# Storing the rows of three late attention steps from other buffers, on another DMA queue and at a later place

## The chip, the cores and the metric

The kernel runs on one core of one Trainium2 chip. A core has the engines TensorE (PE; its weight loads are listed as PEld), VectorE (DVE), ScalarE (ACT), GpSimd (POOL) and SyncE (SP). SP computes nothing here: it issues DMAs. ACT and POOL issue DMAs too; all of them are moved by the core's 16 DMA engines. The metric is the device time of one execution in microseconds (us), lower being better.

## The reference

Two blocks follow each other. The first is a linear attention with decay (4 batches, 8 heads, 768 positions, head size 64, blocks of 64), the second a mixture of experts that sends each of the 3072 tokens to one of 8 experts.

```python
for b in range(nb):                                   # attention
    intra = einsum('bhic,bhjc->bhij', qb, kb) * Dmask
    intra = einsum('bhij,bhjd->bhid', intra, vb)
    inter = einsum('bhid,bhde->bhie', qb * lam_pow, kv_state)
    out[:, :, sl] = intra + inter
    kv_state = lam_block * kv_state + einsum('bhsd,bhse->bhde', kb_dec, vb)
x = out.transpose(0, 2, 1, 3).reshape(B * S, H * D)   # 3072 x 512
logits = x @ w_gate
expert_idx = argmax(logits, axis=1)
for e in range(E):                                    # experts
    xe = x[expert_idx == e]
    h = maximum(xe @ w1[e], 0.0)                      # 512 x 1024
    out[expert_idx == e] = gate_w * (h @ w2[e])       # 1024 x 512
```

## The kernel before, in words

**Attention.** The loop over `steps` has 12 steps: step i handles block pair n = i // 2 (128 positions, of 6) of two batches. For each step q, k and v arrive by DMA from SP (512 KB each) in one of five buffers per name, the lists in `homes` (three of the pool `qkv`, two inside the rooms of the expert weights); step i uses buffer i % 5. PE turns q and k, forms scores and products, and keeps the running states. One step later `leave` turns the step's result into rows of x: `rows` writes them with ACT copies to `m.x`, one of the two slots of `x_room`, and `store_rows` stores these 512 KB to the DRAM tensor `xs` with one DMA from ACT's queue. The logits of the gate are formed beside this, `choose`, `ranks` and `put` give each token a place on its expert's list, and POOL writes the places into the DRAM tensor `slots` with small indirect DMAs ("puts", L467).

**Early start of the experts.** In step 8 `load_early` loads the first expert's w1 (`FIRST` is expert 5) in two DMAs of 1 MB from SP (L1121). `gather_early`, called in step 10, has POOL gather the first 256 rows of this expert's list from the rows that steps 0 to 7 stored (two indirect DMAs, L528, tile `list_0a`), held until the scores of step 11 are through. Behind them SP loads the expert's w2, 2 MB (L1140), with a dependency on both gathers:

```python
        behind = nc.sync.dma_start(out=w2t, in_=w2_r[FIRST])
        pin(behind)
        for other in begun:
            tc.add_manual_dep(behind.ins, other.ins.name, ...)
```

**Experts.** Pass "0a" (these 256 rows) starts while the last places are being given: `turn` (L593), `hidden` (L607, whose results ACT brings out at L560), then `outputs_early`. The product with w2 is done with seven block products instead of eight, from sums: `second_sums` has DVE form four sums of w2 (L684, tiles t_q, t_v, t_k, t_m), `left_of` four sums of the hidden rows (L753 to L756, tiles h_sd, h_qT, h_kT, h_kd), and `block` multiplies (L775): first two products with w2 itself, then t_k with h_kT, t_v with h_sd, and so on. Pass "0b" takes the rest of expert 5 (`list_0b`), and passes 1 to 7 take the other experts; the order of these is computed on the chip (`turns`), so SP reads `turns`, then each list (L497), then issues the loads of w1 (L202) and w2 (L204). The first other expert's rows are gathered by POOL (L528), cut into 16-bit planes by ACT (L576), turned by DMA transposes from SP (L578), joined by ACT (L586) and summed by DVE (L714); the gathers read all of `xs`, so they come after every store of rows.

**Order.** Each engine runs its instructions in order; `pin` keeps an instruction at its written place. All DMAs that SP issues stand in one queue, all that ACT issues in another, POOL's indirect ones in a third.

## Time and profile before

| | |
|---|---|
| median of 3 runs | 432.62 us (432.19 to 433.0) |
| profiled execution, its own time | 432.71 us |
| its span in the profile | 430.9 us |
| PE busy | 420.1 us (97% of the span) |
| PEld / DVE / ACT / POOL busy | 91% / 62% / 41% / 59% |
| granted TensorE clock, mean | 0.993 |
| DMA | 83.11 MB, 193 GB/s over the span |

The span is what the profiler sees from the first to the last instruction; 1.8 us of the execution's time lie around it. The profile names instructions by line, engine, output and input tile. "Idle before" an instruction is the time in which its engine did nothing just before it, put down to what ended last. A DMA's row on SPq or ACTq is its issue alone; the transfer itself shows in the waits for it and in the DMA share and GB/s of a stretch.

### The profile page before, as it was taken

To read this page: it belongs to the slowest core of one execution; us is meant where nothing else is said; L and a number is where in the kernel's file an instruction comes from. 1 tells how busy PE (TensorE), PEld (TensorE's weight loads), DVE (VectorE), ACT (ScalarE), POOL (GpSimd) and SP (SyncE) were. 2 spreads that over 40 slices of the span, in tenths; PEclk is the share of its full clock that TensorE was granted. 3 is DMA by queue.
4 is the path that set the end of the run, shared out by engine and by line. 5 is a ranking of instruction groups with operands and counts; after the bars stand their busy time and mean duration, and the time that the engine had idled before them with its cause. 6 is when DMAs were issued, how large, how long until landed. Compare 5 with 4: busy or idle time off the path is not lost.

```text
span 430.9 us, 9572 instructions
## 1 busy us (share of the span) xinstructions
PE 420.1 (97%) x3699; PEld 392.5 (91%) x3699; DVE 266.1 (62%) x585; ACT 176.7 (41%) x319; POOL 255.5 (59%) x204
## 2 busy tenths in 40 slices
PE   7999999999999999999999999999999999999993
PEld 5888998888888897999999999999999999999972
DVE  6656566676766547686557756665565564775463
ACT  3366546555542433450554155245424605422221
POOL 4242556472444367777948757693984887749032
PEclk8999999999999999999999999999999999999998
DMA  9999999999594759966378846956965894743121
GB/s 174 206 238 243 241 223 259 250 226 223 198 290 155 229 99 273 291 221 257 60 156 182 325 74 153 351 154 119 311 225 84 202 382 77 159 181 56 20 83 63
DMA packets 164551, 83.11 MB, mean 193 GB/s; under 512 B 145923, under 2 KB 145959, under 8 KB 164496
## 3 DMA queue, kind: packets, MB, share of 16 engines
q1 hardware_dynamic: 155024, 63.21, 61.0%
q0 software_dynamic: 5536, 12.88, 9.8%
q10 hardware_dynamic: 3936, 6.31, 4.2%
q8 instruction: 31, 0.51, 0.5%
q14 instruction: 24, 0.20, 0.2%
HBM read 58.96 MB, written 12.72 MB: 166 GB/s over the span
## 4 chain that ended last, share of the span: by engine, by line
PE 93%; ACT 1%; DVE 1%; DMA 1%; SPq 1%; issue 1%; POOL 0%; POOLq 0%
PE p L729 30%; PE p L915 26%; PE sp L279 6%; PE op L314 5%; PE ph L607 5%; PE p L775 4%; PE p L783 3%; PE tx L376 3%; PE cp L340 3%; PE op L305 2%; PE tk L241 2%; PE tq L241 2%; PE lgT L366 2%; DMA k_in<-in_k_dram 1%; ACT xT L332 1%; SPq L114 1%
## 5 line engine op out<-in xcount | busy, mean ns | idle before, releaser
L534 POOL DMA_INDIRECT out_dram<-o_room,list x24 | 25.2, 1048 | 52.2 <-DMA decay<-planes_q 28.3
L286 DVE TENSOR_TENSOR mt<-sp,decay 128x512 f32<-128x512 f32 x48 | 30.1, 684 | 22.4 <-PE sp L279 17.2
L740 ACT ACTIVATE hT<-hT 128x418 f32<-128x418 f32 (+6 forms) x56 | 28.3, 521 | 34.0 <-DVE hT L737 29.9
L729 PE MATMUL p<-xgT,w1t 128*128 128x209 f32 (+6 forms) x224 | 41.4, 327 | 0.0
L729 PEld LDWEIGHTS p<-xgT,w1t 128*128 128x128 f32 x224 | 37.1, 189 | 0.8 <-issue 0.8
L619 ACT COPY u_qT<-p 128x418 f32<-128x418 f32 (+6 forms) x14 | 6.7, 479 | 69.2 <-PE p L729 69.2
L915 PE MATMUL p<-hT,w2t 128*128 128x209 f32 (+5 forms) x192 | 33.6, 328 | 0.0
L915 PEld LDWEIGHTS p<-hT,w2t 128*128 128x128 f32 x192 | 32.0, 189 | 0.0
L528 POOL DMA_INDIRECT xg<-xs,list x25 | 26.3, 1053 | 9.0 <-issue 6.1
L467 POOL DMA_INDIRECT slots<-entry,slot_i x24 | 23.7, 990 | 11.8 <-PE tl L391 5.7
L737 DVE TENSOR_TENSOR hT<-p,u_kd 128x418 f32<-128x418 f32 (+6 forms) x28 | 15.7, 559 | 20.8 <-PE p L729 20.8
L279 PE MATMUL sp<-qT,kT 64*128 64x128 f32 x384 | 27.0, 289 | 0.1
L656 POOL TENSOR_TENSOR s_q<-w1t 128x1024 f32<-128x1024 f32 x7 | 16.5, 2363 | 16.8 <-DVE t_xT L714 14.8
L269 POOL TENSOR_TENSOR kd<-k_in,kdec 128x512 f32<-128x512 f32 x12 | 12.4, 1041 | 23.6 <-issue 10.7
L279 PEld LDWEIGHTS sp<-qT,kT 64*128 64x128 f32 x384 | 23.9, 196 | 2.6 <-issue 2.0
L607 PE MATMUL ph<-xgT,w1t 128*128 128x256 f32 (+1 forms) x128 | 21.6, 328 | 0.0
L326 ACT COPY xT<-op 128x512 f32<-128x512 f32 x12 | 7.0, 585 | 34.8 <-PE op L314 31.2
L586 ACT COPY xgT<-decay 128x1672 uint16<-128x1672 uint16 (+6 forms) x7 | 13.6, 1938 | 17.9 <-DMA decay<-planes_k 9.4
L607 PEld LDWEIGHTS ph<-xgT,w1t 128*128 128x128 f32 x128 | 19.2, 191 | 1.7
L729 PE MATMUL p<-t_sd,w1t 128*128 128x209 f32 (+6 forms) x112 | 20.7, 327 | 0.0
L729 PE MATMUL p<-st,s_q 128*128 128x209 f32 (+6 forms) x112 | 20.7, 327 | 0.0
L653 POOL TENSOR_TENSOR w1t<-w1t 128x1024 f32<-128x1024 f32 x7 | 20.3, 2901 | 0.6
(252 smaller groups left out, 1097.0 us busy)
## 6 DMA issues: line engine op xcount, KB each, us to landing
w2t<-in_moe_w_dram SPq DMA_DIRECT2D x8, 2048.0 KB
w1t<-in_moe_w_dram SPq DMA_DIRECT2D x7, 2048.0 KB
xs<-x_room ACTq DMA_DIRECT2D x12, 512.0 KB
v_in<-in_v_dram SPq DMA_DIRECT2D x8, 512.0 KB
o_room<-qs_room SPq DMA_DIRECT2D x76, 48.0 KB
q_in<-in_q_dram SPq DMA_DIRECT2D x7, 512.0 KB
k_in<-in_k_dram SPq DMA_DIRECT2D x7, 512.0 KB
room<-in_q_dram SPq DMA_DIRECT2D x4, 512.0 KB
```

The source lines that it names most:

```text
L241: pin(nc.tensor.transpose(t[:, i, b, :], src[:, b, h:h + 2, :], ident))
L279: m.scored = pin(nc.tensor.matmul(sp[u][:, i, b, :], lhsT=m.kT[s][halves[u], i, b, :], rhs=m.qT[s][halves[u], i, b, :], start=(i == 0 and ...
L286: nc.vector.tensor_mul(mt[:, u], sp[u], decay[:, u, s * HP // 2:(s + 1) * HP // 2].unsqueeze(2).to_broadcast(shp))
L314: pin(nc.tensor.matmul(out_at(m, b, u, hp), lhsT=m.v[:, b, 2 * hp + u, :], rhs=m.mt[hp // 2][:, u, hp % 2, b, :], start=(first and hp == 0 ...
L467: put = nc.gpsimd.indirect_dma_start(out=slots, out_offset=bass.IndirectOffsetOnAxis(ap=slot_i[:, i:i + 1], axis=0), in_=entry[:, n, bs[i] ...
L528: return nc.gpsimd.indirect_dma_start(out=dst, out_offset=None, in_=xs[:rows, :], in_offset=bass.IndirectOffsetOnAxis(ap=idx, axis=0))
L534: put = nc.gpsimd.indirect_dma_start(out=out, out_offset=bass.IndirectOffsetOnAxis(ap=idx, axis=0), in_=src, in_offset=None, bounds_check= ...
L607: nc.tensor.matmul(ph, lhsT=w1t[:, dc, fc * P:(fc + 1) * P], rhs=m.xgT[:, dc, :], start=(dc == 0), stop=(dc == DC - 1))
L653: return nc.gpsimd.tensor_tensor(out=o, in0=x, in1=y, op=ALU.add)
L729: nc.tensor.matmul(p[:, i, :], lhsT=lhs[:, dc, g, i * P:(i + 1) * P], rhs=rhs[:, dc, :], start=(dc == 0), stop=(dc == DH - 1))
L740: pin(nc.scalar.activation(outs[i][k], outs[i][k], ACT.Relu))
L915: nc.tensor.matmul(p[:, c, :], lhsT=lhs[:, f, c * P:(c + 1) * P], rhs=rhs[:, f, :], start=(f == 0), stop=(f == FC // 2 - 1))
```

## The change

The rows of steps 8, 9 and 10 are no longer copied to `x_room`. They go to the third buffer of q, of k and of v (`homes[name][2]`), whose last user was step 7. Their stores are not issued from ACT one step after each: `store_rows` puts them on a list, and the new `load_behind`, called in step 11, issues all three from SP, in front of the load of the first w2. The dependency on both early gathers now stands on each of the four DMAs. `gather_early` no longer issues that load. The rows of the other nine steps go the old way; as three steps no longer take a slot of `x_room`, the two slots change roles from step 11 on.

```diff
-    def store_rows(m):
+    def store_rows(m, queue=None):
         r0 = 1 + (m.n * B + m.b) * C
-        nc.scalar.dma_start(out=xs[r0:r0 + 2 * C, :].rearrange("(b p) d -> p b d", b=2), in_=m.x)
+        if queue is None and steps.index((m.n, m.b)) in late_rooms:
+            late_stores.append(lambda: store_rows(m, nc.sync))
+            return
+        return (queue or nc.scalar).dma_start(
+            out=xs[r0:r0 + 2 * C, :].rearrange("(b p) d -> p b d", b=2), in_=m.x)
...
-        m.x = x_room[:, next(x_slots)]
+        step = steps.index((m.n, m.b))
+        if step in late_rooms:
+            m.x = late_rooms[step]
+        else:
+            m.x = x_room[:, next(x_slots)]
...
+    late_rooms = {8 + j: homes[name][2].rearrange("p b h d -> p b (h d)")
+                  for j, name in enumerate("qkv")}
+    late_stores = []
...
     def gather_early(other):
-        m, w2t = passes[0], weights[0][1]
+        m = passes[0]
         pin(nc.gpsimd.memset(between, 0.0))
         begun = fetch(m, 1 + (NSTEP - 2) * B * C, pin)
         hold(begun[0], other)
-        behind = nc.sync.dma_start(out=w2t, in_=w2_r[FIRST])
-        pin(behind)
-        for other in begun:
-            tc.add_manual_dep(behind.ins, other.ins.name, mybir.DependencyInfo(
+        early_begun.extend(begun)
+
+    early_begun = []
+
+    def load_behind():
+        w1t, w2t = weights[0]
+        first = [] + late_stores
+        for load in first + [lambda: nc.sync.dma_start(out=w2t, in_=w2_r[FIRST])]:
+            behind = pin(load())
+            for other in early_begun:
+                tc.add_manual_dep(behind.ins, other.ins.name, mybir.DependencyInfo(
...
             else:
+                load_behind()
                 rest()
                 turn(passes[0], pin)
```

On SP, from the loads of the first w1 on, the order before was this (w2t is the first expert's w2, list_0b the list of pass 0b, list_2269 that of the next expert, whose w1 is the last row):

```order
L1121 DMA w1t<-in_moe_w_dram 128x2x1024 x2
L1140 DMA w2t<-in_moe_w_dram 128x8x512
L1257 TENSOR_LOAD turns
L1257 ISA x2
L1320 TENSOR_LOAD beyond
L1320 ISA x2
L497 DMA list_0b<-slots 128x4
L497 ISA
L497 DMA list_2269<-slots 128x4x4
L202 ISA
L202 DMA w1t<-in_moe_w_dram 128x4x1024
```

With the change it is this:

```order
L1134 DMA w1t<-in_moe_w_dram 128x2x1024 x2
L389 DMA xs<-q_in 128x2x512
L389 DMA xs<-k_in 128x2x512
L389 DMA xs<-v_in 128x2x512
L1161 DMA w2t<-in_moe_w_dram 128x8x512
L501 DMA list_0b<-slots 128x4
L1279 TENSOR_LOAD turns
L1279 ISA x2
L501 ISA
L501 DMA list_2269<-slots 128x4x4
L202 ISA
L202 DMA w1t<-in_moe_w_dram 128x4x1024
```

Three stores stand between the loads of w1 and w2, and the scheduler has put the read of list_0b in front of the reads of `turns` and `beyond`, of which `beyond` now stands behind the load of w1.

On ACT, around the rows of step 10 (tx is the turned result in PSUM, xT the result before turning, L386 the store), before:

```order
L382 COPY x_room<-tx 128x512
L1090 COPY parts<-lgT 128x256
L379 COPY x_room<-tx 128x4x64 x2
L386 DMA xs<-x_room 128x2x512
L326 COPY xT<-op_2068 128x4x128
```

With the change:

```order
L382 COPY v_in<-tx 128x512
L1098 COPY parts<-lgT 128x256
L379 COPY v_in<-tx 128x4x64 x2
L326 COPY xT<-op_2064 128x4x128
```

The copies go to another tile and the store is gone from between them; the same holds for steps 8 and 9. The rows of PE, DVE and POOL stand in the same order in both kernels.

## Rows read from the trace of the kernel before

**Rows 1.** The page: the span, and busy time of each engine with its share of the span.

```profile
span 430.9 us, 9572 instructions
PE 420.1 (97%) x3699; PEld 392.5 (91%) x3699; DVE 266.1 (62%) x585; ACT 176.7 (41%) x319; POOL 255.5 (59%) x204
```

**Rows 2.** Busy time by stretch. The columns are the stretch, its length, busy time and instructions of PE, PEld, DVE, ACT and POOL, the granted TensorE clock, the mean busy share of the DMA engines, and what they moved in GB/s.

```profile
80.00:120.00 40.00, 39.43 (x672) 34.16 (x675) 26.18 (x90) 20.57 (x46) 19.63 (x27) 1.00 0.88 224
120.00:126.00 6.00, 5.94 (x76) 4.51 (x64) 3.96 (x24) 3.75 (x11) 1.57 (x3) 1.00 0.91 267
126.00:136.00 10.00, 10.00 (x49) 8.81 (x48) 6.06 (x27) 2.24 (x6) 4.69 (x8) 1.00 0.50 168
136.00:150.00 14.00, 14.00 (x69) 12.32 (x68) 9.17 (x18) 5.29 (x11) 6.00 (x6) 1.00 0.77 259
150.00:170.00 20.00, 19.67 (x148) 16.83 (x146) 10.85 (x27) 5.24 (x6) 14.84 (x11) 1.00 0.67 158
```

**Rows 3.** The waits of SP's own queue between 118 and 145 us: who waited, for what, us in total, times, longest us.

```profile
SPq L1140 <- DMA xg<-xs,list_0a: 16.8, 1, 16.8
SPq L497 <- DMA slots<-entry,slot_i: 3.5, 1, 3.5
```

**Rows 4.** The timeline of DMA issues and of the early gathers: start, us, engine, line, tiles. ACTq L386 are the stores of the rows of steps 8, 9, 10 and 11.

```profile
100.07 0.37 ACTq L386 DMA_DIRECT2D xs<-x_room  x1
110.66 0.37 ACTq L386 DMA_DIRECT2D xs<-x_room  x1
117.43 0.97 POOL L528 DMA_INDIRECT xg<-xs,list_0a  x1 [0.31 <-issue]
119.55 0.37 ACTq L386 DMA_DIRECT2D xs<-x_room  x1
120.99 0.37 SPq L1140 DMA_DIRECT2D w2t<-in_moe_w_dram  x1
124.27 0.37 ACTq L386 DMA_DIRECT2D xs<-x_room  x1
```

**Rows 5.** The timeline of DVE from 129.4 to 141.5 us: the four sums of w2, the four of the hidden rows, the first result of the products.

```profile
132.93 1.23 DVE L684 TENSOR_TENSOR t_q<-w2t 128x1024 f32<-128x1024 f32 x1 [3.51 <-DMA w2t<-in_moe_w_dram]
136.46 1.22 DVE L684 TENSOR_TENSOR t_m<-w2t,t_k 128x1024 f32<-128x1024 f32 x1
137.60 0.70 DVE L753 TENSOR_TENSOR h_sd<-hT 128x512 f32<-128x512 f32 x1
138.73 0.69 DVE L754 TENSOR_TENSOR h_qT<-hT 128x512 f32<-128x512 f32 x1 [0.43 <-ACT hT L560]
139.46 0.69 DVE L755 TENSOR_TENSOR h_kT<-h_qT,hT 128x512 f32<-128x512 f32 x1
```

**Rows 6.** The timeline of PE's weight loads from 137 to 143 us: the products with w2 itself and the first that needs a sum.

```profile
137.90 3.43 PEld L775 LDWEIGHTS p<-w2t,hT 128*128 128x128 f32 x16
141.35 1.70 PEld L775 LDWEIGHTS p<-t_k,h_kT 128*128 128x128 f32 x8
```

**Rows 7.** Busy time by stretch again, columns as in rows 2, for the transfers around the load of w2.

```profile
104.00:112.00 8.00, 8.00 (x110) 6.98 (x108) 5.68 (x19) 5.51 (x12) 2.50 (x5) 1.00 1.03 334
120.50:122.00 1.50, 1.50 (x16) 1.33 (x13) 0.96 (x4) 1.23 (x4) 0.00 (x0) 1.00 0.93 336
122.00:124.00 2.00, 2.00 (x30) 1.54 (x29) 1.45 (x10) 1.82 (x5) 0.00 (x0) 1.00 0.90 138
124.00:130.00 6.00, 5.94 (x31) 4.84 (x30) 4.54 (x36) 1.48 (x6) 5.00 (x9) 1.00 1.01 368
130.00:131.00 1.00, 1.00 (x7) 0.87 (x6) 0.00 (x0) 0.00 (x0) 0.70 (x2) 1.00 0.51 164
131.00:135.00 4.00, 4.00 (x20) 3.54 (x19) 2.07 (x2) 1.23 (x4) 0.57 (x1) 1.00 0.03 3
137.00:144.00 7.00, 7.00 (x34) 6.15 (x34) 5.18 (x9) 0.38 (x1) 4.67 (x5) 1.00 0.99 379
```

**Rows 8.** The timeline of the puts, of the list reads and of what follows from them: POOL, SP and ACT rows, the last two being a DMA transpose of the next expert's rows and the first of their two joins.

```profile
100.53 0.96 POOL L467 DMA_INDIRECT slots<-entry,slot_i  x1 [0.19 <-issue]
109.12 0.78 POOL L497 DMA_DIRECT2D list_0a<-slots  x1 [7.63 <-DMA slots<-entry,slot_i]
130.61 0.96 POOL L467 DMA_INDIRECT slots<-entry,slot_i  x1 [0.30 <-issue]
133.56 0.34 SPq L497 DMA_DIRECT2D list_0b<-slots  x1
153.72 1.27 SPq L578 DMA_TRANSPOSE decay<-planes_k  x1
158.03 2.07 ACT L586 COPY xgT<-decay 128x1672 uint16<-128x1672 uint16 x1 [8.54 <-PE ph L607]
```

**Rows 9.** The timeline of ACT from 128 to 133 us: two of the hidden results of pass 0a.

```profile
131.32 0.38 ACT L560 ACTIVATE hT<-ph 128x256 f32<-128x256 f32 x1 [2.98 <-remote]
132.81 0.38 ACT L560 ACTIVATE hT<-ph 128x256 f32<-128x256 f32 x1 [1.11 <-PE ph L607]
```

**Rows 10.** Busy time by stretch, columns as in rows 2, at the two ends of the span.

```profile
4.00:8.00 4.00, 3.12 (x13) 1.61 (x13) 3.95 (x13) 1.53 (x3) 1.06 (x1) 1.00 1.25 225
8.00:12.00 4.00, 3.74 (x33) 3.41 (x35) 2.57 (x6) 0.81 (x2) 1.04 (x1) 0.57 1.40 215
426.00:428.00 2.00, 0.00 (x0) 0.00 (x0) 0.00 (x0) 0.00 (x0) 0.00 (x0) 1.00 0.30 90
```

More of the change, by code (lines that the diff above doesn't have):

```diff
@@ L1139, in gather_early @@
         hold(begun[0], other)
-        behind = nc.sync.dma_start(out=w2t, in_=w2_r[FIRST])
-        pin(behind)
-        for other in begun:
-            tc.add_manual_dep(behind.ins, other.ins.name, mybir.DependencyInfo(
-                mybir.DependencyClass.Sync, mybir.DependencyReason.DATA),
-                reason="the gathers have the DMA engines first")
+        early_begun.extend(begun)
[7 more added lines that the diff above has]
+                tc.add_manual_dep(behind.ins, other.ins.name, mybir.DependencyInfo(
+                    mybir.DependencyClass.Sync, mybir.DependencyReason.DATA),
+                    reason="the gathers have the DMA engines first")
     with tc.issue_after(keys_made.ins):
```

## The prediction, made before the changed kernel was run

> **What bounds the kernel now.** Start with the page's busy times: PE is busy for 420.1 of 430.9 us [rows 1]. Nothing that leaves PE alone moves the time, so go to the busy time by stretch where the change is made, from step 8 (80 us) to the second pass. From 80 to 120 us PE is idle for 0.57 us, from 120 to 126 us for 0.06, from 126 to 150 us not at all, from 150 to 170 us for 0.33 [rows 2]. That is 0.96 us in 90. What PE could win here is known and small; what it could lose has to be read from the slacks. For that take the queues: SP stands for 16.8 us with the first w2 in hand, until the early gathers have landed [rows 3], and issues it at 120.99 us [rows 4]. DVE then stands idle for 3.51 us until w2 is there at 132.93 us [rows 5]. So w2 is late already for DVE, and the question is how much later it may come before PE feels it.
>
> **The slack of w2.** DVE runs its eight sums in order. The four of w2 and h_sd follow without a hole; before h_qT it waits 0.43 us for ACT; h_kT ends at 139.46 + 0.69 = 140.15 us [rows 5]. PE takes it at 141.35 us, after the two products that use w2 itself and start at 137.90 us [rows 6]. If w2 lands D later, the wait of 0.43 us is filled first, and h_kT ends at 139.72 + D. PE stands still from D = 141.35 - 139.72 = 1.6 us on; I take off 0.1 for the semaphore: **1.5 us of slack**. The products with w2 itself have 137.90 - 132.93 = 5.0 us and are not the first to stop. Behind the first stall the whole row of products moves as one; PE has no idle time in the stretch that follows [rows 2], so a stall of S there is S at the end.
>
> **What is taken away.** Three issues of 0.37 us leave ACT's queue, at 100.07, 110.66 and 119.55 us [rows 4]. ACT is busy for 20.57 of 40 us from 80 to 120 us [rows 2]: worth nothing. The copies of the rows cost what they did, since only their target changes. The two other copies to `x_room` no longer share its slots with steps 8 to 10; no row shows a wait for a slot, so nothing. 1 MB (steps 8 and 9) leaves the stretch from 100 to 116 us, where the DMA engines are full (1.03 from 104 to 112 us [rows 7]). A put issued at 100.53 us lands so late there that the read of list_0a waits 7.63 us [rows 8]. It would come earlier now, but the gathers are held for PE's scores, so this earliness buys nothing. What is left is PE's 0.57 us of idle time before 120 us [rows 2], of which a part may be DMA pressure: between nothing and -0.57; I take nothing, as PE waits for no DMA there. The store of step 10 was issued at 119.55 us, after the last gather's issue had ended at 118.40 [rows 4]; the gathers win next to nothing.
>
> **What is added: 1.5 MB in front of w2.** SP is released at 120.99 us as before and now issues three stores, of 0.37 us each by ACT's rows [rows 4], then w2 at about 122.1 us; that is no cost as long as the stores are still moving. When do they move? Step 10's store was issued at 119.55 us and the engines move data at 336 GB/s from 120.5 to 122.0 us, 0.50 MB, about one store [rows 4, 7]. So data flow 0.9 us after an issue: from 121.9 us. The bytes: three stores are 1.57 MB, w2 is 2.10 MB, and step 11's store (124.27 us, ACT's queue [rows 4]) is 0.52 MB that shares the engines either way. Before, the 2.62 MB of w2 and step 11 took from 122.0 to 130.9 us: slowly at first (138 GB/s up to 124 us), then at 368 GB/s [rows 7], and DVE saw w2 2.0 us after that (132.93 us [rows 5]). I leave these 2.0 us as they are.
>
> - Lower end: all 4.19 MB at the best rate of a row, 379 GB/s: 11.1 us, to 133.0 us, D = 2.1, S = 0.6.
> - Upper end: the stores at 336 GB/s take 4.7 us, to 126.6 us, and w2 then begins just as slowly as before and needs its 8.9 us: 135.5 us, D = 4.6, S = 3.1.
> - Taken: the stores at 336 GB/s, w2 and step 11 at 368 GB/s without a slow beginning: 4.7 + 7.1 = 11.8 us, to 133.7 us, D = 2.8, **S = 1.3**. It is nearest to the row from 104 to 112 us, where loads stand behind other loads in one queue and the rate stays at 334 GB/s without a hole [rows 7].
>
> **The lists behind w2.** The last put was issued at 130.61 us and done issuing at 131.57; with the DMA engines then idle (0.03 [rows 7]) SP read list_0b at 133.56 us, 2.0 us later [rows 8]. Now the engines are full until 133.7 us. The put lands between 133.5 us (no delay) and 139.2 us (7.6 us, as at 100.53 us [rows 8]); I take 2 us after the engines run empty, 135.7 us, 2.1 later. The read of `turns` in front of the next list adds 0.3, an estimate. Gathers, planes and transposes of the next expert thus come 2.4 us later. Their reserve: the last transpose that the first join needs is issued until 154.99 us, and the join begins at 158.03 us, held by PE and not by a transpose [rows 8]: a reserve between 0 and 3.0 us, for the landing takes a part of it. PE itself is 1.3 us later. So this path adds between 0 and 1.1 us; I take 0, since it needs all its reserve to be the landing. In the worst case, 5.6 + 0.3 us without any reserve, it would add 4.6.
>
> **ACT beside it.** One hidden result waits 2.98 us for "remote", until 131.32 us, when the DMA engines have run empty [rows 9, 7]. If that wait ends with the traffic, it ends 2.8 us later, at 134.1 us. It is the third of eight hidden products, and the code has three banks for them, so the sixth has to wait for it. The eighth is through at about 137.9 us; 16 weight loads take 3.43 us [rows 6], so the 8 of one product take 1.7, and the sixth begins at about 132.8 us (an estimate). PE would stand there for 134.1 + 0.4 - 132.8 = 1.7 us. That takes the place of the stall of 1.3 us and does not add to it, since the later products move along: 0.4 us more at the most. I count 0.1.
>
> **Sum.** 432.71 (the profiled execution) + 1.3 + 0 = 434.0 us; with the 0.1 from ACT I say **434.1 us**. The profiled execution lies 0.09 us above the median of the runs, 432.62, so the difference is the same against it. A measurement of this kernel can tell about 0.2%, 0.87 us, from no change; S passes that from D = 2.4 us on.
>
> **The rivals.**
>
> *The stores fill a hole and cost no time that counts.* Place: the slow beginning of w2 from 122 to 124 us, 138 GB/s where 368 are possible, which is room for 0.46 MB [rows 7]. For it: in the new order w2's descriptors are queued while the stores still move. Against it: the rate it needs, 379 GB/s over 11 us, is the best of any row. It decides below D = 2.4 us; at the lower end above, S = 0.6: 433.3 us, no change. The Trainium skill's page "DMA: Bandwidth & Descriptors", section "Anatomy of one DMA", has a transfer's variable part as bytes over 436 GB/s; by that the 4.19 MB would be through at 131.5 us, D = 0.6, no stall at all and 432.7 us. The trace does not bear that out so far: the best of my rows is 379 GB/s [rows 7].
>
> *PE's small holes close.* With 1 MB less between 100 and 116 us and the stores in a hole, the idle 0.57 + 0.06 + 0.33 us [rows 2] could all go: 431.75 us, just at the bound of faster. Against it: PE waits for ACT and its own issue in them, and it needs D below 1.5 too.
>
> *w2 begins slowly again, or the lists become the bound.* The upper end gives 432.71 + 3.1 = 435.8 us. A put that lands as late as the one at 100.53 us gives, with half of the reserve, 5.9 - 1.5 = 4.4, or 437.1 us. For it: before, the slow beginning stood right behind a store as well, that of step 10 [rows 4, 7]. Against it, for the lists: the engines are full for only 2 us past the last put's issue, and for 8 us in the other place.
>
> *TensorE's clock falls in the stall.* From 8 to 12 us the granted clock was 0.57 after a stretch in which PE was busy for 3.12 of 4 us [rows 10]; 4 us at that clock cost 1.7 us against full clock, 435.8 us in all. Against it: at the end of the span PE is wholly idle from 426 to 428 us and the clock still stands at 1.00, 2.4 GHz [rows 10]; and a stall of 1.3 us is shorter.
>
> **How the numbers follow.** Forecast (433.6 to 434.9 us): 0.45. Stores in the hole (433.3, down to 432.7): 0.24. Closed holes: 0.09, of which two thirds below 431.75 with the spread of a measurement. Slow w2 or late lists: 0.19. Clock: 0.03. Faster by over 0.2% is 0.06; within 0.2% is 0.24 + 0.03 = 0.27; slower is 0.45 + 0.19 + 0.03 = 0.67. The range goes from 432.5 (half of the hole rival's cases and the spread of the runs) to 436.0 (the upper end of w2), leaving out some 2 in 10; the forecast's own range is 433.6 to 434.9 us.
>
> **What would show it.** Right: SP's three stores from about 121.0 us, w2 at about 122.1; DVE's wait in front of t_q grows from 3.5 to about 6.3 us and t_q starts near 135.7; PE stands for 1.3 us in front of the product with t_k and h_kT, and nowhere else; the DMA engines are full to 133.7 us. Wrong: t_q before 135.0 us (the hole rival); a stall of PE in front of the next expert's first products near 165 us, with the joins waiting for transposes (the lists); a granted clock under 1 after 142 us (the clock); fewer PE holes before 120 us (the closed holes). If t_q is late as said and PE doesn't stall, the slack was read wrongly.

## The result, and the profile after

| | before | after |
|---|---|---|
| median of the runs | 432.94 us (432.19 to 434.25, 6 runs) | 437.07 us (436.16 to 438.2, 6 runs) |
| ratio | | 1.0086, 95% interval 1.0068 to 1.0105 |
| profiled execution | 432.71 us, span 430.9 | 436.57 us, span 434.8 |

The change costs 4.1 us. The direction was forecast, the size was not: 434.1 us was forecast, with a range up to 436.0. In two later comparisons on other chips the change cost 3.2 and 3.0 us (ratios 1.0063 [1.0034, 1.0092] and 1.0056 [1.003, 1.0082]), so 3 to 4 us is what has to be explained.

The page of the profile after: the work on PE is what it was (420.1 us before), the span is 3.9 us longer [rows 1].

```profile
span 434.8 us, 9582 instructions
PE 420.5 (97%) x3699; PEld 392.6 (90%) x3699; DVE 261.7 (60%) x585; ACT 176.8 (41%) x319; POOL 255.3 (59%) x204
```

Busy time by stretch, with the columns of [rows 2]. PE loses 2.47 us from 136 to 150 us and 0.98 us from 150 to 170, where it lost nothing and 0.33. The granted clock (the third number from the end) stays at 1.00.

```profile
80.00:120.00 40.00, 39.34 (x683) 34.28 (x683) 25.87 (x89) 20.48 (x46) 19.70 (x27) 1.00 0.84 206
120.00:126.00 6.00, 5.94 (x61) 4.47 (x54) 4.11 (x27) 3.95 (x12) 1.89 (x3) 1.00 0.75 250
126.00:136.00 10.00, 10.00 (x48) 8.81 (x47) 2.83 (x23) 1.99 (x6) 4.40 (x8) 1.00 0.99 272
136.00:150.00 14.00, 11.53 (x54) 9.83 (x53) 10.69 (x17) 1.91 (x4) 5.35 (x5) 1.00 0.68 235
150.00:170.00 20.00, 19.02 (x143) 15.98 (x143) 10.07 (x26) 7.73 (x10) 12.54 (x9) 1.00 0.57 119
```

PE stands in two places. These are rows of the timeline of its weight loads; the bracket is the idle time before the row and what ended it:

```profile
143.88 1.59 PEld L779 LDWEIGHTS p<-t_k,h_kT 128*128 128x128 f32 x8 [2.88 <-DVE h_kT L759]
154.24 6.78 PEld L611 LDWEIGHTS ph<-xgT,w1t 128*128 128x128 f32 x60 [0.76 <-ACT xgT L604]
170.46 1.36 PEld L733 LDWEIGHTS p<-st,s_q 128*128 128x128 f32 x8 [0.16 <-POOL s_q L660]
```

The first is the stall that was forecast, 2.88 us instead of 1.3. The second is in the hidden products of pass 0b, which no forecast had. The third row is the first product of the next expert that needs a sum made by POOL. It waits for next to nothing, but it starts 3.35 us later than before: most of the 3.9 us of the span can be read there.

**Two paths are late.** The first is w2's. SP issues what was forecast, at 120.70 to 122.58 us, but w2 is with DVE at 137.15 us instead of 135.7:

```profile
120.70 0.37 SPq L389 DMA_DIRECT2D xs<-q_in  x1
122.58 1.21 SPq L1161 DMA_DIRECT2D w2t<-in_moe_w_dram  x1
136.72 0.34 SPq L501 DMA_DIRECT2D list_0b<-slots  x1
138.56 0.41 SPq L501 DMA_DIRECT2D list<-slots  x1
149.16 1.33 SPq L582 DMA_TRANSPOSE decay<-planes_q  x1
```

```profile
137.15 1.23 DVE L688 TENSOR_TENSOR t_q<-w2t 128x1024 f32<-128x1024 f32 x1 [8.04 <-DMA w2t<-in_moe_w_dram]
143.14 0.69 DVE L759 TENSOR_TENSOR h_kT<-h_qT,hT 128x512 f32<-128x512 f32 x1
```

The second path is that of the lists. The read of list_0b (third row of the SP block) waits for the last put and is issued at 136.72 us, 3.2 us later than before [rows 8]. From there the delay is passed on: to POOL's gathers of the next expert, ACT's planes, SP's transposes. ACT's copy of the turned rows of pass 0b stands behind the planes in ACT's order, and that copy is what PE waits 0.76 us for.

```profile
139.36 1.00 POOL L532 DMA_INDIRECT xg<-xs,list_0b  x1 [8.09 <-DMA list_0b<-slots]
163.31 0.99 POOL L532 DMA_INDIRECT xg<-xs,list  x1 [3.45 <-DMA list<-slots]
168.02 2.38 POOL L660 TENSOR_TENSOR s_q<-w1t 128x1024 f32<-128x1024 f32 x1
```

```profile
148.51 1.14 ACT L580 COPY planes_q<-xg 128x512 uint16<-128x512 uint16 x2 [10.13 <-DMA xg<-xs,list]
153.83 0.36 ACT L604 COPY xgT<-tp 128x256 f32<-128x256 f32 x1
```

**Why w2 is late: the rate.** Busy time by stretch from 121.5 us, the last two numbers being the share of the DMA engines and GB/s:

```profile
121.50:125.00 3.50, 3.44 (x37) 2.44 (x35) 2.82 (x20) 2.41 (x8) 1.08 (x2) 1.00 0.99 356
125.00:128.50 3.50, 3.50 (x19) 3.04 (x20) 2.76 (x24) 0.94 (x3) 2.93 (x6) 1.00 0.99 234
128.50:132.00 3.50, 3.50 (x18) 3.07 (x17) 0.54 (x3) 0.38 (x1) 2.28 (x4) 1.00 1.07 359
132.00:134.00 2.00, 2.00 (x11) 1.77 (x10) 0.00 (x0) 0.66 (x2) 0.00 (x0) 1.00 1.08 148
134.00:136.00 2.00, 2.00 (x11) 1.77 (x10) 0.00 (x0) 0.38 (x1) 0.00 (x0) 1.00 0.80 295
```

The stores run at 356 GB/s (336 was forecast). Then the engines are busy all the time but move 234 GB/s for 3.5 us, and later 148 GB/s for 2 us. The 4.19 MB take from 121.5 to 136.0 us, 289 GB/s in the mean; the 2.62 MB of before had 294 GB/s in the mean (8.9 us). A byte more in front cost what a byte had cost before.

### The profile page after: what moved, and what is told of

It is laid out like the page before. It is cut to its first block, busy times and chain, and to the rows that moved or that the text cites. A ratio compares the mean times of both kernels' runs of the same rounds, so it can differ in the third digit from the quotient of the medians.

```text
span 434.8 us, 9582 instructions
## 1 busy us (share of the span) xinstructions
PE 420.5 (97%) x3699; PEld 392.6 (90%) x3699; DVE 261.7 (60%) x585; ACT 176.8 (41%) x319; POOL 255.3 (59%) x204
## 4 chain that ended last, share of the span: by engine, by line
PE 85%; DMA 4%; ACT 3%; DVE 3%; issue 2%; POOL 1%; SPq 1%; POOLq 0%; ACTq 0%; DVEq 0%
PE p L733 30%; PE p L919 26%; PE sp L279 6%; PE op L314 5%; PE tx L376 3%; PE cp L340 3%; PE op L305 2%; PE tk L241 2%; PE tq L241 2%; PE ph L611 2%; DMA xg<-xs,list 2%; PE p L787 2%; PE lgT L366 2%; DMA slots<-entry,slot_i 1%; DMA k_in<-in_k_dram 1%
## 5 line engine op out<-in xcount | busy, mean ns | idle before, releaser
L611 PE MATMUL ph<-xgT,w1t 128*128 128x256 f32 (+1 forms) x128 | 21.9, 329 | 0.6 <-ACT xgT L604 0.6
L733 PE MATMUL p<-t_xT,w1t 128*128 128x209 f32 (+6 forms) x112 | 20.6, 326 | 0.0
```

The costliest lines, as they stand in the source:

```text
L611: nc.tensor.matmul(ph, lhsT=w1t[:, dc, fc * P:(fc + 1) * P], rhs=m.xgT[:, dc, :], start=(dc == 0), stop=(dc == DC - 1))
L733: nc.tensor.matmul(p[:, i, :], lhsT=lhs[:, dc, g, i * P:(i + 1) * P], rhs=rhs[:, dc, :], start=(dc == 0), stop=(dc == DH - 1))
```

## The experiments

The theory at the outset (w2, "theory 1" below): the loss is the lateness of w2, less a slack of some 1.6 us. The rival (lists): the loss is the lateness of the lists behind it. A third (clock) came up on the way.

**What is not the cause.** In rooms_only the three rows go to the other buffers, but ACT stores them as before: the lines that put the store on the list are taken out.

> The rows of steps 8, 9 and 10 go to the third buffers of q, k and v, but their stores are issued from ACT one step later, as before. Theory 1 (the bytes in front of w2 make it late, and PE stalls from 1.5 us on): w2 as early as before, t_q near 132.9 us, no stall, the same as before within 0.2%. Rival (the other buffers or the changed slots of x_room cost something by themselves): 1 to 4 us slower.

433.32 us against 432.69, ratio 1.0008 [0.9987, 1.0028]. The other buffers and the changed slots of `x_room` cost nothing that can be measured.

**How the loss grows.** The set of late steps is cut down, in late_10 to the last of the three, in late_9_10 to the last two.

```diff
-                  for j, name in enumerate("qkv")}
+                  for j, name in enumerate("qkv") if j > 1}      # late_9_10: if j > 0
```

> Only step 10's rows are stored late, from SP in front of w2; steps 8 and 9 as before. Theory 1: 0.52 MB that stood in front of w2 already, from ACT's queue, now start 1.4 us later: t_q 1 to 1.5 us later than before, which the slack of 1.5 us takes up: the same as before within 0.2%, no wait of PE for h_kT above 0.3 us. Rival (it is the place on SP's queue behind the gathers, or the lists behind it, that costs, whatever the size): 1 us slower or more.

> Steps 9 and 10 are stored late, step 8 as before: 1.05 MB in front of w2 on SP. Theory 1: at 350 GB/s t_q comes 1.5 us later than with one store, some 2.8 us later than before; PE waits 1.3 us for h_kT; 1.2 to 1.6 us slower than before, a third to a half of the loss with three stores. Rival (lists): the loss does not go with the wait for h_kT.

late_10: 432.8 us, 1.0001 [0.9989, 1.0014], no stall in front of h_kT's product. late_9_10: 433.95 us, 1.0029 [1.0019, 1.0039], with a stall of 1.06 us. t_q comes 0.4 us later with one store in front of w2 (1 to 1.5 was expected), 2.7 with two and 4.5 with three (each counted from PE's first hidden product of pass 0a). So the stall begins at 2.7 - 1.06 = 1.6 us of lateness, as it does in the change (4.5 - 2.88 = 1.65): the slack was read rightly, within 0.15 us.

**Bytes or writes.** before_loads is the kernel before with three loads of 512 KB, into the same buffers and behind the same gathers, in front of w2; no row is moved.

```diff
-        behind = nc.sync.dma_start(out=w2t, in_=w2_r[FIRST])
-        pin(behind)
-        for other in begun:
+        for load in loads + [lambda: nc.sync.dma_start(out=w2t, in_=w2_r[FIRST])]:
+            behind = pin(load())
+            for other in begun:
```

> The kernel before with three loads of 512 KB from the inputs into the free buffers of step 7 in front of w2 on SP; their data is not used, and the stores of rows stay at ACT as before. Theory 1 (bytes in front of w2 at the mean rate of this stretch): t_q 4 to 5 us later than before, PE waits 2.5 to 3.3 us for h_kT, 2.5 to 4 us slower than before. Rival (it is the writes to DRAM, or their change to reads, that is slow): 1.57 MB of loads at 368 GB/s, step 10's store ahead of them as well, t_q at most 4 us later and no slow stretch between the loads and w2.

436.94 us, ratio 1.0091 [1.0068, 1.0113], the loss of the change. t_q is 4.0 us late and PE stalls for 2.38 us. 1.5 MB in front of w2 and of the lists is enough for the loss; that the new transfers are stores into DRAM is not needed for it. A slow stretch is here as well, behind the loads:

```profile
126.00:128.00 2.00, 2.00 (x11) 1.77 (x10) 1.86 (x16) 0.38 (x1) 1.62 (x4) 1.00 0.76 175
```

**Taking w2 out of the way.** In w2_half_early, half of w2 is loaded right behind w1 and the other half behind the stores; in half_only the same is done to the kernel before. In w2_first, w2 stands in front of the stores.

```diff
# w2_half_early, in load_early; half_only has the same line
+        pin(nc.sync.dma_start(out=w2t[:, :FC // 2], in_=w2_r[FIRST][:, :FC // 2]))
# w2_first, in load_behind
-        first = [] + late_stores
-        for load in first + [lambda: nc.sync.dma_start(out=w2t, in_=w2_r[FIRST])]:
+        first = [lambda: nc.sync.dma_start(out=w2t, in_=w2_r[FIRST])]
+        for load in first + late_stores:
```

> The change with half of w2 (1 MB) loaded straight behind w1, in the stretch in which the DMA engines run empty before the gathers; the other half behind the three stores. Theory 1: 1 MB less behind the stores takes some 3 us off: t_q near 134 us, no wait for h_kT, 0 to 0.6 us slower than before. Rival (the stores make the lists late, and these set the end): 1.5 us slower or more although w2 is in time, with PE waiting in front of the next expert's products.

> The kernel before, with one edit: the first half of w2 (1 MB) is loaded right behind the two loads of w1, and only the second half stands behind the gathers. No row of steps 8 to 10 is moved. If w2 was late without cost in the kernel before (1.65 us of slack and no stall), the half that comes early brings nothing: 432.2 to 433.4 us, t_q about 129, PE without a wait in front of h_kT. If the early half brings something that the three late stores then used up in the version with both, this one is faster than that: 431.0 to 432.0 us.

> The change with w2 in front of the three stores on SP, all else alike. Theory 1: nothing stands in front of w2, t_q at 132 to 133 us, no wait of PE for h_kT. The stores end near 136 us, though, and the gathers behind them, which read all rows, start near 139 us as with the change: the next expert's planes come 3 to 4 us later than before with no stall of PE to hide it, so its first products wait 1 to 2.5 us: 1 to 2.5 us slower than before, less than the change. Rival (w2 is not it, only the lists): as slow as the change, 3.7 us. Rival (w2 is all there is): the same as before within 0.2%.

w2_half_early takes 432.82 us, 1.0005 [0.9996, 1.0014]: the loss is gone. That doesn't yet tell the paths apart, since 1 MB less behind the gathers brings the lists in time as well (list_0b is read at 133.60 us); t_q is at 129.02 us, where 134 was expected. half_only takes 433.26 us, 1.0 [0.9988, 1.0013]: w2 earlier than before brings nothing, as its lateness of before cost nothing. No version here beats the kernel before.

w2_first decided against the w2 theory. It has w2 in time and no wait in front of h_kT's product, and yet it takes 439.24 us, 1.0153 [1.0134, 1.0172], 6.2 us more than before and worse than the change. DVE, POOL and PEld in its timeline:

```profile
132.00 1.22 DVE L688 TENSOR_TENSOR t_q<-w2t 128x1024 f32<-128x1024 f32 x1 [2.69 <-issue]
139.72 1.17 POOL L532 DMA_INDIRECT xg<-xs,list_0b  x1 [8.25 <-DMA list_0b<-slots]
154.33 8.40 PEld L611 LDWEIGHTS ph<-xgT,w1t 128*128 128x128 f32 x60 [3.38 <-ACT xgT L604]
```

The lists are as late as in the change, and PE now pays for it in front of pass 0b, 3.38 us. I had put 1 to 2.5 us on this for the lists; that was too little. 1.6 us of the rest are the clock, which fell behind that wait (60 loads in 8.40 us, 6.78 in the change).

**Taking the lists out of the way.** no_puts leaves out the last six puts, which makes the lists free to be read early; w2_first_no_puts does that with w2 in front. In both, the first gather of pass 0b is held behind the last of SP's DMAs that follow the early gathers (w2, or the last store); it starts at 137.29 and 137.35 us, 139.36 in the change.

```diff
-    store_places_behind(turned_back, len(waiting))
     give_places(*give_ranks())
-    store_places(len(waiting), lambda inst: inst)
+    waiting.clear()
...
-        fetch(m)
+        begun = fetch(m)
+        if m is passes[1]:
+            hold(begun[0], w2_load[0])
```

> The change without the last six puts (the places of the last six groups are not written, so their tokens are on no list); the first gather behind them waits for w2 instead, so that it stays out of w2's way. Theory 1: the puts do not matter, t_q near 137 us, PE waits 2.5 to 2.9 us for h_kT. Rival (the small writes of the puts make the slow stretches around 126 and 133 us): t_q 1.5 us earlier or more, the wait at most 1.3 us, and no stretch at 100 to 200 GB/s with full engines.

> w2 in front of the three stores on SP, and the last six puts left out (so the tokens of the last six groups are on no list; the lists keep their sizes), with the first gather of the second pass held until SP's waits for the early gathers are over. t_q is in time (132 us) in any case. If the late list is what costs 6.2 us in the version with w2 first, the list is read near 130.5 us, the gathers start near 137 us, behind the stores instead of the list, planes_q starts near 144 us, PE waits less than 0.5 us in front of the second ph of pass 0b, and the time is 433 to 434.5 us. If it is the stores that hold the gathers, or a put has no part in it, planes_q starts at 147 us or later, PE waits 2 us or more, and the time is 436 to 439 us.

no_puts: 434.44 us, 1.0038 [1.0022, 1.0055], a loss of 1.4 us, which is w2's alone. t_q is 3.0 us late and the stall is 1.33 us. w2_first_no_puts: 432.75 us, 0.9996 [0.9983, 1.001]. With w2 in time and the lists in time nothing is lost, though the three stores move as late as in w2_first; the 6.2 us of w2_first were the lists' alone, with the fall of the clock behind their wait. no_puts also tells what the second slow stretch was. Its rows of 125 to 136 us:

```profile
125.00:128.50 3.50, 3.44 (x19) 2.65 (x18) 2.87 (x27) 0.77 (x4) 0.00 (x0) 1.00 0.91 215
132.00:134.00 2.00, 2.00 (x11) 1.77 (x10) 0.00 (x0) 0.66 (x2) 0.00 (x0) 1.00 1.05 405
134.00:136.00 2.00, 2.00 (x11) 1.77 (x10) 0.00 (x0) 0.45 (x2) 0.00 (x0) 1.00 1.11 364
```

The first stretch, 215 GB/s, is still there, so the puts do not make it. I read it as w2's own slow beginning, since before it stood at w2's beginning too, ahead of the store of step 11 [rows 4, 7]; here that store begins in the same stretch, and no run separates the two. The second has gone from 148 to 405 GB/s: that was the puts.

**The stores on ACT's queue.** act_queue has w2 on SP as before, and the three late stores issued by ACT behind that of step 11.

```diff
-            late_stores.append(lambda: store_rows(m, nc.sync))
+            late_stores.append(lambda: store_rows(m, nc.scalar))
...
     store_rows(last)
+    for load in late_stores:
+        pin(load())
```

> The three stores are issued from ACT right behind step 11's, at about 125 us, and w2 from SP at 121 us with nothing in front. Theory 1 with shared engines (both queues move at once): w2 gets about half of the rate from 125 us on, t_q 3 to 4 us later than before, PE waits 1.5 to 2.5 us for h_kT, 1.5 to 3.5 us slower than before. Rival (it is the place in front of w2 in SP's queue): t_q at most 1 us later, no wait, the same as before within 0.3%.

443.5 us, 1.0234 [1.0209, 1.026], far beyond both expectations. With the stores pinned there, the scheduler put DVE's places of the last tokens among the sums of w2, and the last two puts went out some 8.6 us late (8.75 us of idle time in front of the first, where the change has 0.19):

```profile
138.13 0.96 POOL L471 DMA_INDIRECT slots<-entry,slot_i  x1 [8.75 <-DVE slot_i L469]
```

So its time says nothing of queues; it is the hardest case of late lists, and serves as such in the table below. For w2 itself the run does answer the question:

```profile
125.87 0.72 ACTq L389 DMA_DIRECT2D xs<-v_in  x1
132.16 1.23 DVE L688 TENSOR_TENSOR t_q<-w2t 128x1024 f32<-128x1024 f32 x1 [2.74 <-DMA w2t<-in_moe_w_dram]
```

All three stores are issued by 126.6 us, beside w2, and yet t_q starts 8.3 us after PE's first hidden product of pass 0a (9.25 before), and PE does not wait for h_kT. So 1.5 MB beside w2, on another queue, did not make it late in this execution, as the rival had it, while 1.5 MB in front of it on SP did (the change, before_loads). Two puts fewer ran beside the load than in the change.

**The chain of the lists to its end.** The late read of list_0b can reach PE a second time, one pass on. ACT's planes come late, so SP's eight transposes of them start late; they follow each other without a hole, and behind them SP reads the lists of the next pass, POOL gathers by those, and only behind these gathers POOL forms s_q, which PE needs. In the kernel before, the rows are these (the gathers are the first and the last of four; the fifth row, DVE's last sum of the next expert's rows, is explained below the table):

```profile
145.60 1.32 SPq L578 DMA_TRANSPOSE decay<-planes_q  x1
159.87 0.99 POOL L528 DMA_INDIRECT xg<-xs,list  x1 [2.44 <-DMA list<-slots]
163.78 0.88 POOL L528 DMA_INDIRECT xg<-xs,list  x1 [0.31 <-issue]
164.68 2.38 POOL L656 TENSOR_TENSOR s_q<-w1t 128x1024 f32<-128x1024 f32 x1
163.83 0.59 DVE L714 TENSOR_TENSOR t_xT<-xgT,st 128x418 f32<-128x418 f32 x1
167.11 1.36 PEld L729 LDWEIGHTS p<-st,s_q 128*128 128x128 f32 x8 [0.15 <-POOL s_q L656]
```

POOL's gathers ended at 164.66 us, s_q followed at 164.68, and PE waited 0.15 us for it: this path had no reserve. The first transpose and the product with s_q in the profiled executions:

| | list_0b read | first transpose | PE's product with s_q | from one to the other |
|---|---|---|---|---|
| before | 133.56 | 145.60 | 167.11 | 21.5 |
| rooms_only | 134.03 | 145.70 | 167.60 | 21.9 |
| late_10 | 134.69 | 146.14 | 167.57 | 21.4 |
| late_9_10 | 135.38 | 146.81 | 168.26 | 21.5 |
| before_loads | 136.34 | 148.98 | 170.48 | 21.5 |
| the change | 136.72 | 149.16 | 170.46 | 21.3 |
| w2_first | 137.22 | 149.94 | 171.97 | 22.0 |
| act_queue | 141.66 | 154.38 | 175.80 | 21.4 |
| no_puts | early | 143.83 | 168.73 | 24.9 |
| w2_first_no_puts | early | 143.68 | 167.74 | 24.1 |

Over a spread of 8.8 us, with w2 late or in time, the product stands 21.3 to 22.0 us behind the first transpose. Only where the lists are early does something else clearly set it (there POOL's s_q waits 2.32 us for DVE's t_xT). In the change the first transpose is 3.56 us later than before and the product 3.35 us: nearly all of the 3.9 us of the span. The stall for w2 stands inside this time; it does not add to it.

The lists are not alone at s_q, though. The code (`finish` in `first_sums`) holds s_q until t_xT is done as well, and t_xT follows PE's own hidden products of pass 0b, through ACT's joins. In rooms_only, w2_first and the two versions without puts, s_q starts 0.15 us (0.16 in one) behind the end of t_xT, so PE's own row sets it there and not the lists; w2_first pays for its lists at the copy of xgT. In the change the row is this:

```profile
167.10 0.67 DVE L718 TENSOR_TENSOR t_xT<-xgT,st 128x418 f32<-128x418 f32 x1
```

s_q starts at 168.02 us, 0.25 behind its end; before it was 0.26. So in this execution PE's own row, late by the stall for w2 and the wait for xgT, and the lists come to s_q together, the lists by 0.1 us the later. They are later by 0.6 us in change_again_2, 1.2 in change_again_4 and 0.7 in late_9_10. Of PE's own delay in the change, 0.76 us, the wait for xgT, comes from the lists too.

**The clock.** The rival of a falling clock was seen in no row of the first profile, but before_loads showed 0.59 and 0.56 from 144 to 148 us:

```profile
144.00:146.00 2.00, 2.00 (x7) 1.60 (x6) 1.38 (x4) 0.00 (x0) 1.52 (x2) 0.59 1.01 414
146.00:148.00 2.00, 2.00 (x7) 1.62 (x6) 0.24 (x1) 0.00 (x0) 0.00 (x0) 0.56 1.07 410
```

So the change was profiled again, and two versions kept PE busy in the stall, with ten and with five more matmuls on operands that are there already.

```diff
+        for x, y in fill:                       # in block; fill_stall: ten, fill_half: five
+            nc.tensor.matmul(p, lhsT=x, rhs=y, start=True, stop=True)
```

> The changed kernel once more, for another profiled execution: six executions lie between 436.16 and 438.20 us, and the one profiled has a granted clock of 1.00 from 120 us to the end. If TensorE's clock falls behind the stall in some executions, one of the slower ones shows a granted clock under 1 between 140 and 160 us and a time of 437 to 438.5 us. If the stall never costs clock, both look like the first, 436 to 436.8 us, or are slower by a longer stall alone.

> The same as the run before it, a second execution: clock theory, a granted clock under 1 between 140 and 160 us where the time is over 437 us; stall theory, a time that follows the stall of PE in front of h_kT and of the second ph of pass 0b alone, with the clock at 1.00.

> The changed kernel with ten more matmuls (128x128 by 128x256, 0.22 us each) in front of the product with t_k and h_kT, with operands that are there already and a result that the product overwrites. They fill 2.2 of PE's 2.3 to 2.5 us of idle time; w2 is as late as in the change and h_kT ends no sooner. Clock theory (the clock falls because PE stands idle there): the granted clock is 1.00 from 120 us to the end, the product with t_k takes about 1.9 us, and the median is 436.0 to 436.9 us, some 0.5 to 1.7 us under the change on the same chip. If the fall has another cause (the heavy DMA traffic, the load of w2), the clock falls as before and the median is that of the change, 437 to 438 us.

> The changed kernel once more, timed beside the filled one: 436.2 to 438.2 us, in two groups if the clock falls in some executions alone (436.2 to 436.8 without, 437.4 to 438.2 with); the granted clock under 1 between 140 and 152 us where the profiled one is over 437 us.

> A second profiled execution of the filled kernel. Clock theory: 1.00 from 120 us on again, 436.0 to 436.9 us. Otherwise: a granted clock of 0.8 to 0.9 between 140 and 152 us, over 437 us.

The weight loads of the product with t_k in change_again_2, and the stretches around it:

```profile
143.97 3.06 PEld L779 LDWEIGHTS p<-t_k,h_kT 128*128 128x128 f32 x8 [2.67 <-DVE h_kT L759]
```

```profile
144.00:146.00 2.00, 2.00 (x5) 1.64 (x6) 1.84 (x4) 0.00 (x0) 1.39 (x3) 0.50 1.02 408
146.00:148.00 2.00, 2.00 (x8) 1.64 (x7) 0.61 (x2) 0.00 (x0) 0.66 (x1) 0.71 1.00 391
```

The clock is at 0.50, 1.2 GHz, behind the stall, and the product takes twice its time. This was so in three of the five profiled executions of the change, after PE had stood for 2.2 to 2.4 us (PE's own rows; 2.0 in before_loads). It was not so in the other two, after 2.5 and 1.8 us, so the length alone does not tell. The time does not tell either: 435.53 us with the fall, 436.57 without. In both executions of fill_stall the clock behind that place stays at 1.00. But its median is 436.5 us beside 435.61 of the change: no gain. It is not a clean test, though: the ten matmuls took 4.3 us, 0.43 each, where I had reckoned 0.22, and pushed the product some 1.5 us past the end of h_kT (142.74 us). These are the two products with w2 itself, the ten, and the product with t_k:

```profile
136.46 3.43 PEld L783 LDWEIGHTS p<-w2t,hT 128*128 128x128 f32 x16
139.91 4.29 PEld L781 LDWEIGHTS p<-w2t,hT 128*128 128x128 f32 x20
144.23 1.70 PEld L783 LDWEIGHTS p<-t_k,h_kT 128*128 128x128 f32 x8
```

> The changed kernel with five more matmuls (0.43 us each, 2.15 us in all) in front of the product with t_k and h_kT: they fit into PE's idle time of 2.3 to 2.5 us and push nothing back. Clock theory: granted clock 1.00 from 120 us on, the product with t_k takes 1.9 to 2.0 us, and the median lies 0.5 to 1.7 us under that of the change beside it (the fall was seen in three of four executions and takes 1.7 us where it is seen; where it is not, up to 0.8 us is lost to the lists instead, so the gain may be as small as 0.5). If the fall only takes time that the lists would take anyway, the medians agree within 0.3 us though the clock stays up.

> The changed kernel beside the filled one: PE idle for 2.3 to 2.5 us in front of the product with t_k; in three of four executions, so probably here, a granted clock of 0.8 to 0.9 behind it and 2.6 to 3.6 us for that product; 2.9 to 4.5 us over the kernel before.

> A second profiled execution of fill_half: clock theory 1.00 from 120 us on; otherwise 0.8 to 0.9 somewhere between 140 and 152 us.

Five matmuls fit into the stall. The clock behind it is 1.00 in both executions again, and again there is no gain: 436.71 us (434.91 to 441.04) beside 435.58. Both filled versions lie about 1 us above the change, with intervals that overlap; what that is was not followed. In fill_half_again PE's weight load waits only 0.36 us for h_kT, but 3.17 us at the end of the chain of the lists:

```profile
142.39 1.59 PEld L783 LDWEIGHTS p<-t_k,h_kT 128*128 128x128 f32 x8 [0.36 <-DVE h_kT L761]
152.97 6.78 PEld L611 LDWEIGHTS ph<-xgT,w1t 128*128 128x128 f32 x60 [0.98 <-ACT xgT L604]
172.13 2.59 PEld L735 LDWEIGHTS p<-st,s_q 128*128 128x128 f32 x8 [3.17 <-POOL s_q L662]
```

Behind this later wait the clock falls too, to 0.61 over 8 us, and this execution takes 440.64 us:

```profile
172.00:180.00 8.00, 7.87 (x27) 7.66 (x28) 1.52 (x3) 4.34 (x9) 5.70 (x4) 0.61 1.04 392
```

The executions of the change itself fit this. The table has each wait of PEld in us, and the way from the first transpose to the product with s_q:

| | time | for h_kT | clock behind it | for xgT of 0b | for s_q | from the first transpose |
|---|---|---|---|---|---|---|
| the change | 436.57 | 2.88 | 1.00 | 0.76 | 0.16 | 21.3 |
| change_again_1 | 437.95 | 2.56 | falls | none | 0.16 | 21.3 |
| change_again_2 | 437.87 | 2.67 | falls | none | 0.67 | 21.7 |
| change_again_3 | 435.53 | 2.77 | falls | none | 0.15 | 21.7 |
| change_again_4 | 435.58 | 2.18 | 1.00 | 1.23 | 1.27 | 21.9 |

Where the clock falls, PE is later and the two waits behind it shrink. The way to s_q is no longer with the fall than without it. The fall behind the stall is real and costs nothing that these runs can tell, since in all five executions the lists hold s_q back for longer than PE's own row, by 0.1 to 1.2 us. Elsewhere it costs time, as in w2_first.

## Why the prediction was wrong, point by point

- **Where PE would stall, and the slack of w2**: right. PE stalls in front of the product with t_k and h_kT, from 1.6 us of lateness on (1.5 forecast).
- **What is taken away**: right at nothing. PE was busy 39.34 us from 80 to 120 us, 39.43 before [rows 2]; rooms_only has no effect.
- **1.5 MB in front of w2**: a size was off. The step that failed is "w2 and step 11 at 368 GB/s without a slow beginning": D was 4.5 us instead of 2.8, so S 2.9 instead of 1.3. The upper end of that step, 4.6 and 3.1, hits the measured size, but in part by luck. Its reason, that w2 begins slowly again, holds: a slow stretch stays behind other transfers, 234 GB/s here, 175 behind the loads of before_loads. But that explains a D of 3.0 and an S of 1.33, as without the puts; the other 1.5 us are the puts, which the sum didn't have. The Trainium skill's page "DMA: Bandwidth & Descriptors", section "Anatomy of one DMA", which gives its rate for DMAs that GpSimd issues, would have had the 4.19 MB through at 436 GB/s; this case's trace, of DMAs that SP issues, does not agree: 289 GB/s. Its section "Specifications" says that transfers under 512 B make the engine read and write back; that fits the puts, and beyond the gap of 148 to 405 GB/s no run here shows it.
- **The lists behind w2**: this is the other step that failed, and its mechanism was wrong, "I take 0, since it needs all its reserve to be the landing". The lateness was not far off (2.1 us forecast for the read of list_0b, 3.2 measured), the reserve was. I took it from the join, which PE holds and not a transpose [rows 8], and stopped there. But the transposes are also what SP's next list reads stand behind, and through POOL's gathers they hold s_q. The gathers that end just before s_q starts, and that product's row with its wait of 0.15 us for POOL, were in the trace of before and I had not looked for them. With a reserve of nothing, 2.4 us of forecast lateness would have given 2.4 us there, and 435.1 us; the 3.56 us measured give 436.3, beside 436.57 in the profiled execution. The second way, through ACT's order to the copy of xgT, was not in the forecast either: 0.76 us in the change, 3.38 in w2_first.
- **The sum**: I took the larger of the two delays as if the path of w2 were the longer. The runs show two paths side by side: w2's alone costs 1.4 us (no_puts, at a D of 3.0), that of the lists alone 6.2 us with w2 in front (1.6 of it the clock), both relieved nothing. They do not add. No run has the lists in time at the change's D of 4.5; by the stall, w2's path alone would cost some 2.9 us there, an estimate.
- **The rivals**: "slow w2 or lists" had this outcome, at 435.8 to 437.1 us, and 0.19 was too little for it. The stores did not fill a hole, and PE's small holes did not close. The fall of the clock was put down too easily at 0.03: it is there in three of five executions, and it was wrong to infer from a stretch at the end of the span that a short stall is safe. That it hardly moves the time of the change is due to the lists.
- **ACT beside it**: a wait of hT for "remote" is there, 1.83 us until 132.61 us, but PE does not stand for it; ACT delayed PE in another place, with the copy for pass 0b behind the planes.

Open: in the last two comparisons PE reaches pass 0a some 1.3 us sooner in the changed kernel (122.2 us instead of 123.5 to 124.7), and the loss there is 1 us smaller; what of that belongs to the chip was not separated. Nor were the last 0.5 us of the span followed (3.35 us at the product with s_q, 3.9 at the end).

## What to carry to other kernels

A reserve is the least of all ways from the late transfer to the busy engine, and a way may lead through the orders of three queues into the next pass: follow each row that a late transfer delays until it meets a wait of the bound engine, and there compare the end of that row's engine with the start of what the bound engine takes from it: s_q followed the gathers by 0.02 us, which says that the path has no reserve left. Ask also what else held that row; here it hung on the bound engine itself. Bytes put in front of an urgent load are priced at the mean rate that the same stretch had with its slow beginnings and small writes, not at the rate of its best row. Where two paths are late, relieve each by itself before adding them up: the visible stall here, and the clock behind it, could both be filled without any gain.

## What the runs showed of the hardware that was not expected

- Six puts of small pieces (the last issued at 130.31 us) beside a 2 MB load that still moves afterwards: from 132 to 134 us the engines stay busy (1.08) and move 148 GB/s, against 405 without the puts. Before, w2 was through by then, and while the same puts were issued it moved at 368 GB/s [rows 7]. The read that waits for the last put was issued 6.4 us after the put (130.31 to 136.72 us), 3.0 us in the kernel before.
- The slow beginning of a 2 MB load did not hide behind transfers in front of it: 138 GB/s for 2 us before [rows 7], 234 GB/s over 3.5 us behind three stores with the engines busy (0.99), 175 GB/s for 2 us behind three loads. What of the second is the store of step 11 is not separated.
- Three stores of 512 KB, issued from ACT's queue while a 2 MB load from SP's moved, did not make that load late (act_queue): t_q stood 8.3 us behind PE's first hidden product, 9.25 before.
- TensorE's clock between 0.50 and 0.71 (at 1.2 GHz for a part of the time) in the stretches of 2 us from 144 to 148 us, behind 2.0 to 2.4 us of standing still, in four of six executions (the change and before_loads; the other two stood for 1.8 and 2.5 us and kept 1.00), and at 1.00 behind that place in the four executions in which other matmuls filled the time.
